# A fused Fourier-filter and ELU-MLP kernel: order of the k2 = 0 products and place of one unit's sums, against buffers, engines and places of the opening's last pieces

## The chip, the cores and the metric

One NeuronCore of a Trainium2 chip runs the whole kernel in one launch. The metric is the device time of one execution in microseconds (us); lower is better. The engines are PE (TensorE; PEld is its weight loads), DVE (VectorE), ACT (ScalarE), POOL (GpSimd) and SP (SyncE, which here only issues DMAs). ACT and POOL issue DMAs as well.

## The reference, cut to what matters

```python
# x: (8, 3008, 256) float32; filt_r, filt_i: (1505, 256) float32
X = np.fft.rfft(x, axis=1)
y = np.fft.irfft(X * (filt_r + 1j * filt_i)[None], n=3008, axis=1).astype(np.float32)
t = y.reshape(8 * 3008, 256)
h = t @ w_in                                  # w_in: (256, 2048) float64
g = np.where(h > 0.0, h, np.exp(np.minimum(h, 0.0)) - 1.0)
out = (g @ w_out).astype(np.float32)          # w_out: (2048, 256) float64
```

A real Fourier transform over 3008 positions, a product with a filter for each frequency and channel, the transform back, and then a two-layer network with ELU between the layers.

## The kernel before, in words

**Transform.** 3008 = 47 x 64, so each transform is done in two steps, with tables of sines and cosines as matmul weights: forward `a_unit` (64) and `b_unit` (47, then the products with the filter on DVE), back `bi_unit` (47) and `n_unit` (64). Between them the intermediate results go through DRAM: `z_write` and `z_read` before `b_unit`, `y_write` and `y_read` (tensor `yd`) before `n_unit`. A batch b has 8 groups g of 4 frequencies k2, and 6 units m of output positions. From the second batch on, `bi_unit` takes two groups at once: 16 products of 32x32 tiles of PE, with row strip 32a and column strip 32p for a, p = 0 to 3, whose inputs (`zs`, z) GpSimd has added up in lines 385 to 395. For g = 0 the frequency k2 = 0 needs weights of its own, so each of the four tiles with a = 0 does two products of half the width (lines 405 to 411). Before, these come as: the four special halves, the twelve other tiles, the four ordinary halves. ACT copies the four results out (line 412).

**The first batch** has forms of its own, `a_first`, `t_first`, `b_first`, `bi_first`, `y_write_first`, which keep the data on the core as far as they can. `bi_first` (line 347) puts the result of group g into one half, g % 2, of one tile `t3f`; ACT fills it (lines 356, 357) and `y_write_first` writes it to `yd` by two DMAs (line 364), for the last group one of them from ACT's queue. Then `y_read(0, 0)` (line 430), two DMAs from SP and two from ACT, reads what `n_unit(0, 0)` needs (line 443 on PE, line 445 the copies by ACT).

**Network.** Both layers multiply in seven products in place of eight, on blocks of two by two. `combine` (lines 469 to 472) forms the sums of the input blocks of one unit on DVE. An item is (b, m, q), q a quarter of the hidden width. `up_steps` does seven products of two matmuls each (line 494), with copies by ACT (line 505) and adds by DVE (line 502), ELU by two ACT operations (lines 511, 512) and one of DVE (line 516), and at the end four sums on DVE (lines 552 to 556). `down_steps` does the seven products of the second layer one item later (line 576). `c_unit` (line 592) combines those of four quarters on DVE, `o_unit` turns them and writes them out.

**Weights.** They arrive as 64-bit numbers in 16 pieces k = 0 to 15 and are turned into 32-bit ones on the core: `w_fetch` (DMA, line 650), `w_split` (DVE, lines 662, 663), `w_float` (ACT: lines 670, 671 and, in `w_power`, 678, 679), `w_join` (DVE, lines 685 to 698). After each second piece `w_sums` (lines 706 to 709) forms the block sums of four operations on DVE. The 15th piece is k = 14; pieces 14 and 15 use the same working tiles.

**Order.** Everything is issued in an order written out by hand; each engine does its own instructions in the order in which the program names them, and waits where data or a buffer is not yet free. After the opening a loop runs over quads i: quad i holds the up steps of item i and the down steps of item i - 1, mixed by a string of U and D. A table `plan` holds what else is issued: at place 0, after the first four up steps, or at place 1, after the tails of the quad. Batch b begins at quad (b - 1) * 24, and unit m = 5 has its first up step at 44 behind that. In that loop before, `n_unit` of m = 5 comes at quad 40, place 0, and its sums, split off as `n_sums`, at quad 41, place 1; the other units have both at one place. PSUM has four banks that all these units share in turn and four for the second layer.

Of the kernel before, what the change touches and what calls it, by code (L numbers as in the profile page):

```python
# [11 lines left out]
FP32 = mybir.dt.float32  # L12
U32 = mybir.dt.uint32
AXT = mybir.ActivationFunctionType
ALU = mybir.AluOpType
# [11 lines left out]
P = 128  # L27
D = 256
# [6 lines left out]
NG = K2 // 4  # L35
# [93 lines left out]
def kernel(  # L129
# [9 lines left out]
    nc = tc.nc  # L139
# [6 lines left out]
    def pool(name, bufs, **kw):  # L146
        return ctx.enter_context(tc.tile_pool(name=name, bufs=bufs, **kw))
# [7 lines left out]
    t2p = pool("t2p", 2)  # L155
# [13 lines left out]
    bb = pairs[:, P:3 * P].rearrange("p (v a i) -> p v a i", v=2, a=4)  # L169
# [8 lines left out]
    xs, tas, tns, t1s, t2s, ss, t3s, t4s, zs, yds, ys, g_of, po_of, cs_, sds = ({} for _ in range(15))  # L178
# [8 lines left out]
    def bank(name, shape=(P, 2, D)):  # L187
        i = banks.pop(0)
        return i, psM.tile(list(shape), FP32, tag="m%d" % i, name=name)
# [156 lines left out]

    def bi_first(g):
        s = ss.pop((0, g))
        t = t3s[0, g] = t3f[:, g % 2]

        pa, pb = (psO.tile([P, 2, 256], FP32, tag="po%d" % i, name="po%d" % i)
                  for i in ((0, 1) if g > 2 and g % 2 else (2, 3)))
        for o, table, sv in ((0, gr, s[0]), (64, gi, s[1])):
            for ps, k in ((pa, LO), (pb, HI)):
                tile_mm(ps[o:o + 64], table, k, sv, g == 0 and k == LO)
        nc.scalar.activation(out=t[:, 0:2, :], in_=pa, func=AXT.Copy)
        nc.scalar.activation(out=t[:, 2:4, :], in_=pb, func=AXT.Copy)
# [41 lines left out]
    def bi_unit(b, g):  # L399
        z = ss.pop((b, g))  # L400
        t = t3s[b, g] = t3p.tile([P, 2, 4, D], FP32, tag="t3", name="t3")
        pv = [bank("pv") for _ in range(4)]

        both = [(p, a, slice(1 if g == a == 0 else 0, 2), 0) for p in range(4) for a in range(4)]
        if g == 0:
            both = [(p, 0, slice(0, 1), 1) for p in range(4)] + [w for w in both if w[1]] + [w for w in both if not w[1]]
        for p, a, js, v in both:
            r = slice(32 * a, 32 * a + 24)
            nc.tensor.matmul(pv[a][1][32 * p:32 * p + 32, js, :], bb[r, v, p, :], z[r, p, js, :],  # L409
                             start=True, stop=True, tile_position=(32 * a, 32 * p))  # L410
        for a, (i, ps) in enumerate(pv):
            nc.scalar.activation(out=t[:, :, a, :], in_=ps, func=AXT.Copy)
            banks.append(i)
# [22 lines left out]
    def n_unit(b, m):  # L436
        t, w, h = t4s.pop((b, m)), tns.pop((b, m)), half(m)
        rows = []
        for dh in range(2):
            y = yp.tile([P, 512], FP32, tag="y%d" % dh, name="y%d" % dh)  # L440
            k, ps = bank("psn", (P, 512))
            for q, i in enumerate(order(m)):
                nc.tensor.matmul(ps[:, ts(q, P)], t[:, i - 4 * m, ds(dh * P, P)], w[:, i - 4 * m, :],  # L443
                                 start=True, stop=True)
            nc.scalar.activation(out=y[:, 0:2 * h], in_=ps[:, 0:2 * h], func=AXT.Copy)
            banks.append(k)
            rows += [y[:, 0:h], y[:, h:2 * h]]
        s = yp.tile([P, 3, 256], FP32, tag="ys", name="ys")
        ys[b, m] = rows + [s[:, i, 0:h] for i in range(3)]

    def n_sums(b, m):
        ys[b, m] = combine(*ys[b, m])

# [11 lines left out]
    def combine(b11, b12, b21, b22, t1, t2, t4):  # L467

        nc.vector.tensor_tensor(out=t1, in0=b12, in1=b11, op=ALU.subtract)
        nc.vector.tensor_tensor(out=b12, in0=b22, in1=b12, op=ALU.subtract)  # L470
        nc.vector.tensor_tensor(out=t2, in0=b22, in1=t1, op=ALU.subtract)
        nc.vector.tensor_tensor(out=t4, in0=b21, in1=t2, op=ALU.subtract)
        return {1: b11, 2: b21, 3: b22, 4: t4, 5: t1, 6: t2, 7: b12}
# [191 lines left out]
    def w_float(k, part=None):  # L665
        m, e, f, l = wts[k]
        if part == 1:
            return w_power(e)

        nc.scalar.activation(out=l, in_=wds[k][:, :, 0], func=AXT.Identity, scale=2.0 ** -52)  # L670
        nc.scalar.activation(out=f, in_=m, func=AXT.Identity, scale=2.0 ** -20, bias=1.0)
        if part is None:
            w_power(e)
# [7 lines left out]
    def w_join(k):  # L681
        q, j = divmod(k, 4)
        m, e, f, l = wts.pop(k)
        hi = wds.pop(k)[:, :, 1]
        nc.vector.scalar_tensor_tensor(out=e, in0=hi, scalar=0x80000000, in1=e,
                                       op0=ALU.bitwise_and, op1=ALU.bitwise_or)
        nc.vector.tensor_tensor(out=f, in0=f, in1=l, op=ALU.add)
        e = e.bitcast(FP32)
        if j < 2:
            f, e = (t.rearrange("p (a j c) -> p a j c", a=2, j=2) for t in (f, e))  # L690
            dst = w_in[q][:, 2 * j:2 * j + 2, :, :].rearrange("p j a c -> p a j c")
            nc.vector.tensor_tensor(out=dst, in0=f, in1=e, op=ALU.mult)
        else:

            f, e = (t.rearrange("p (i a e s) -> p i e a s", i=2, a=4, e=2) for t in (f, e))
            dst = w_out[q][:, 0:4, j - 2, :].rearrange("p (i e) (a s) -> p i e a s", i=2, a=4)
            for i in range(2):
                nc.vector.tensor_tensor(out=dst[:, i], in0=f[:, i], in1=e[:, i], op=ALU.mult)
        if j % 2 == 1 and k < 15:
            w_sums(k)  # L700

    def w_sums(k):
        q, j = divmod(k, 4)
        w = (w_in if j < 2 else w_out)[q]
        a11, a21, a12, a22, s1, s2, s4 = (w[:, i] for i in range(7))
        nc.vector.tensor_tensor(out=s1, in0=a21, in1=a22, op=ALU.add)
        nc.vector.tensor_tensor(out=s2, in0=s1, in1=a11, op=ALU.subtract)
        nc.vector.tensor_tensor(out=s4, in0=a12, in1=s2, op=ALU.subtract)
        nc.vector.tensor_tensor(out=a21, in0=a11, in1=a21, op=ALU.subtract)

    def f_arrange():

# [27 lines left out]
    with tc.manual_schedule():  # L740


        with tc.tile_pool(name="boot", bufs=1) as bp:
# [9 lines left out]
            t3f = t3p.tile([P, 2, 4, D], FP32, tag="t3", name="t3")  # L753
# [86 lines left out]
            w_join(12)  # L840
            w_fetch(15)
            w_split(14)
            w_float(14)
            w_join(13)
        for c in range(2):
            x_load(1, c)
# [2 lines left out]
        ep = pool("ep", 2)  # L849
        op = pool("op", 1)  # L850
        n_unit(0, 0)
        n_sums(0, 0)
        w_join(14)

# [3 lines left out]
        def at(quad, place, fn, *a):  # L860
            plan.setdefault((quad, place), []).append((fn, a))


        for quad, place, fn, *a in ((0, 0, w_split, 15), (1, 1, w_float, 15, 0), (2, 0, w_float, 15, 1), (2, 1, w_join, 15),
                                    (3, 0, w_sums, 15)):
            at(quad, place, fn, *a)
        for c in range(2, XBUFS):
# [7 lines left out]
        for b in range(B):  # L875
            t = (b - 1) * PER
            if b > 0:
                for c, s in enumerate((2, 2, 4, 4, 7, 7)):
                    at(t + s, 0, x_unit, b, c)
                    if c % 2 == 0:  # L880
                        opens.add(t + s + 1)
                        at(t + s, 1, a_unit, b, c)
                    nb, nxt = (b, c + XBUFS) if c + XBUFS < NXC else (b + 1, c + XBUFS - NXC)
                    if nb < B:
                        at(t + s, 1, x_load, nb, nxt)
                    at(t + s, 1, z_write, b, c)
                for g in range(NG):
                    s = t + 9 + g + g // 2
                    at(s, 1, b_unit, b, g)
                    at(s - 2, 1, f_read, b, g)  # L890
                    at(s - 2, 1, z_read, b, g)
                    if g % 2:

                        opens.add(s + 2)
                        at(s + 1, 1, bi_unit, b, g - 1)
                        at(s + 1, 1, y_write, b, g - 1)
            for m, (s, place) in enumerate(((23, 0), (25, 1), (29, 1), (32, 0), (36, 0), (40, 0))):
                if b > 0 or m > 0:
                    at(t + s - 2, 0, tn_read, b, m)
                    at(t + s - 2, 0, y_read, b, m)  # L900
                    at(t + s, place, n_unit, b, m)

                    at(*((t + s + 1, 1) if m == 5 else (t + s, place)), n_sums, b, m)
                at(t + PER + 4 * m + 5, 0, c_unit, b, m)
                at(t + PER + 4 * m + 6, 0, o_unit, b, m)

        items = [(b, m, q) for b in range(B) for m in range(6) for q in range(4)]
        for i in range(-PER, len(items) + 3):
# [3 lines left out]
            for k in "DUUDUDDU" if i in opens else "UUDUDDU":  # L912
                s = ups if k == "U" else downs
# [4 lines left out]
            for k in "DUUDUD" if i in opens else "DUUDUDD":  # L918
                s = ups if k == "U" else downs
# [40 lines left out]
```

## Time and profile before

| | us |
|---|---|
| three runs | 2618.73, 2620.72, 2621.56 |
| median | 2620.72 |
| the profiled execution | 2620.72 |
| its span, first to last instruction | 2618.7 |
| busy: PE / DVE / ACT / POOL | 2569.9 / 1852.8 / 1504.0 / 486.9 |
| 20 us stretches of the opening, PE busy: 60 to 80, 80 to 100 | 16.55, 9.95 |
| granted PE clock in those | 0.83, 0.76 |

The profile is of one execution. Times in it count from the span's start. Matmuls are pipelined and their ends are modelled, so a busy PE is not PE at its peak; a line of the timeline gives the start, the duration, the engine, the source line and what is written and read, xN merges N records, and square brackets give the engine's idle time before and what ended it. A float32 matmul is two passes, so two records, each with a weight load of its own. Lines of the list of waits read: who waited for whom, us in total, times, longest. In the chain of waits each piece is what the next one had to wait for.

### The profile page before, as it was taken

The numbers are of one execution on the slowest core, as the hardware profiler recorded it, in microseconds if no ns is written. First come the engines' busy times: TensorE is split into PE (matmuls) and PEld (weight loads), VectorE is DVE, ScalarE is ACT, GpSimd is POOL, SyncE is SP. The second block draws the span as 40 slices with busy tenths as digits, with TensorE's granted clock in tenths as the row PEclk, the third lists the DMA queues.
The fourth block names the chain that finished last, engine by engine and source line by source line (L and its number), as shares of the span: only waits on it lengthen the run. The fifth ranks groups of instructions, "written<-read, shape, count | busy, mean of one in ns | idle before, by whom it ended". The sixth has DMA issues, their size and how long they took to land.

```text
span 2618.7 us, 41226 instructions
## 1 busy us (share of the span) xinstructions
PE 2569.9 (98%) x15300; PEld 2220.2 (85%) x15300; DVE 1852.8 (71%) x3203; ACT 1504.0 (57%) x2622; POOL 486.9 (19%) x669
## 2 busy tenths in 40 slices
PE   6799999999999999999999999999999999999998
PEld 4688889888898888988889888998889888898887
DVE  6876776677666776777667767677677667766666
ACT  7665555655555555555555555555555555555554
POOL 5102330024100331004300134002330023300000
PEclk9899999999999999999999999999999999999999
DMA  9544222432224232333314331143321332210010
GB/s 296 169 115 105 63 63 55 117 83 70 66 62 115 63 92 48 82 90 80 79 45 104 83 98 45 45 111 96 86 61 40 87 85 63 63 41 20 22 28 17
DMA packets 228840, 206.51 MB, mean 79 GB/s; under 512 B 130962, under 2 KB 194674, under 8 KB 228640
## 3 DMA queue, kind: packets, MB, share of 16 engines
q1 hardware_dynamic: 211328, 166.90, 25.4%
q0 software_dynamic: 15856, 36.25, 4.9%
q8 instruction: 121, 1.98, 0.3%
q10 hardware_dynamic: 1456, 0.72, 0.1%
q14 instruction: 79, 0.65, 0.1%
HBM read 131.91 MB, written 78.17 MB: 80 GB/s over the span
## 4 chain that ended last, share of the span: by engine, by line
PE 96%; DMA 0%; DVE 0%; ACT 0%; issue 0%; DVEq 0%; SPq 0%; ACTq 0%
PE po L576 44%; PE phs L494 25%; PE phd L494 12%; PE pha L494 6%; PE psn L443 3%; PE psr L376 2%; PE psa L228 2%; PE pv L409 1%; PE po L324 0%; DMA yd<-t 0%; PE psi L376 0%; DMA t<-yd 0%; PE psr L324 0%; DVE c L592 0%; PE psi L324 0%
## 5 line engine op out<-in xcount | busy, mean ns | idle before, releaser
L576 PE MATMUL po<-g,wo 128*128 128x256 f32 (+1 forms) x5376 | 1306.1, 376 | 0.0
L576 PEld LDWEIGHTS po<-g,wo 128*128 128x128 f32 x5376 | 1016.2, 190 | 139.1 <-issue 20.0
L505 ACT ACTIVATE g<-phs 128x512 f32<-128x512 f32 (+1 forms) x576 | 339.3, 589 | 819.2 <-PE phs L494 819.1
L502 DVE TENSOR_TENSOR g<-phd,g 128x512 f32<-128x512 f32 (+1 forms) x384 | 259.4, 675 | 413.3 <-ACT e L512 322.2
L512 ACT ACTIVATE e<-e 128x512 f32<-128x512 f32 (+1 forms) x768 | 477.2, 621 | 24.3
L516 DVE SCALAR_TENSOR_TENSOR g<-e,g 128x512 f32<-128x512 f32 (+1 forms) x576 | 400.5, 695 | 1.3 <-ACT e L512 1.3
L494 PE MATMUL phs<-y,wi 128*128 128x256 f32 (+1 forms) x1536 | 394.5, 380 | 0.0
L494 PE MATMUL phs<-ys,wi 128*128 128x256 f32 (+1 forms) x1536 | 387.9, 375 | 1.5 <-ACT g L505 1.5
L511 ACT ACTIVATE e<-g 128x512 f32<-128x512 f32 (+1 forms) x576 | 353.2, 613 | 35.7 <-DVE g L502 26.6
L494 PEld LDWEIGHTS phs<-y,wi 128*128 128x128 f32 x1536 | 284.9, 191 | 55.1 <-issue 11.5
L494 PEld LDWEIGHTS phs<-ys,wi 128*128 128x128 f32 x1536 | 291.9, 190 | 34.9 <-ACT g L505 2.5
L385 POOL TENSOR_TENSOR sr<-sr,zs 128x512 f32<-128x512 f32 x56 | 71.3, 1273 | 1131.7 <-DVE zs L330 1131.7
L516 DVE SCALAR_TENSOR_TENSOR g<-e,phs 128x512 f32<-128x512 f32 (+1 forms) x192 | 129.9, 677 | 128.5 <-ACT e L512 128.5
L511 ACT ACTIVATE e<-phs 128x512 f32<-128x512 f32 (+1 forms) x192 | 112.9, 588 | 147.7 <-PE phs L494 147.7
L494 PE MATMUL phd<-ys,wi 128*128 128x256 f32 (+1 forms) x768 | 194.6, 376 | 0.0
L494 PE MATMUL phd<-y,wi 128*128 128x256 f32 (+1 forms) x768 | 193.8, 375 | 0.0
L494 PE MATMUL pha<-y,wi 128*128 128x256 f32 (+1 forms) x768 | 193.8, 375 | 0.0
L494 PEld LDWEIGHTS phd<-ys,wi 128*128 128x128 f32 x768 | 145.4, 190 | 19.0 <-DVE g L502 3.0
L494 PEld LDWEIGHTS pha<-y,wi 128*128 128x128 f32 x768 | 146.1, 190 | 16.3
L494 PEld LDWEIGHTS phd<-y,wi 128*128 128x128 f32 x768 | 146.1, 190 | 16.2
L502 DVE TENSOR_TENSOR g<-pha,g 128x512 f32<-128x512 f32 (+1 forms) x192 | 129.2, 673 | 40.5 <-PE pha L494 40.2
L553 DVE TENSOR_TENSOR g<-g,g 128x512 f32<-128x512 f32 (+1 forms) x192 | 130.7, 681 | 6.7
(129 smaller groups left out, 2356.5 us busy)
## 6 DMA issues: line engine op xcount, KB each, us to landing
yd<-t SPq DMA_DIRECT2D x127, 192.0 KB
t<-yd SPq DMA_DIRECT2D x190, 128.0 KB
z<-t SPq DMA_DIRECT2D x84, 256.0 KB
f<-fp POOLq DMA_DIRECT2D x224, 96.0 KB, 3.1
t<-z SPq DMA_DIRECT2D x224, 96.0 KB
out_dram<-o SPq DMA_DIRECT2D x632, 32.0 KB
tn<-tn_t SPq DMA_DIRECT2D x48, 256.0 KB
xc<-in_x_dram SPq DMA_DIRECT2D x84, 128.0 KB
```

The source lines that it names most:

```text
L228: nc.tensor.matmul(p[o:o + 64, u, :], w[r, u, o:o + 64], src[r, u, :], start=True, stop=True)
L376: nc.tensor.matmul(ps[32 * a:32 * a + 32, c, :], fb[k, 1 if g == a == 0 else 0, c, :], t[k, a, :], start=True, stop=True)
L385: nc.gpsimd.tensor_tensor(out=sr, in0=sr, in1=p, op=ALU.add)
L443: nc.tensor.matmul(ps[:, ts(q, P)], t[:, i - 4 * m, ds(dh * P, P)], w[:, i - 4 * m, :], start=True, stop=True)
L494: nc.tensor.matmul(ps[:, a, 0:h], w_in[q][:, COMBO[n], a, :], y[n], start=start and a == 0, stop=True, skip_group_check=True)
L502: nc.vector.tensor_tensor(out=g[o], in0=i0, in1=i1, op=ALU.add)
L505: nc.scalar.activation(out=g[o], in_=i0, func=AXT.Copy)
L511: nc.scalar.activation(out=e, in_=src, func=AXT.Relu, scale=-1.0)
L512: nc.scalar.activation(out=e, in_=e, func=AXT.Exp, scale=-1.0)
L516: nc.vector.scalar_tensor_tensor(out=g[n], in0=es[n], scalar=1.0, in1=src, op0=ALU.subtract, op1=ALU.max)
L553: nc.vector.tensor_tensor(out=b12, in0=b22, in1=b12, op=ALU.subtract)
L576: nc.tensor.matmul(po[i][:, u, 0:h], w_out[q][:, COMBO[n], a, :], g[n][:, a, :], start=q == 0 and a == 0 and n in (1, 3, 6, 4), stop=True, ...
```

## The change

It does two things at once. It puts in new places for the end of the opening, and it takes back an order of the k2 = 0 products and a split of the sums of the unit m = 5.

- `bi_first`: for g = 6 and 7 the result goes into a tile of its own from the pool `t2p`, not into a half of `t3f`.
- `w_sums`: pieces 11, 13 and 15 on GpSimd, the earlier ones on DVE as before.
- Piece 14: the last two ACT operations of `w_float` move from ahead of `n_unit(0, 0)` to quad 0, place 0; `w_join(14)` from behind the first unit's sums to quad 0, place 1; `w_split(15)` from quad 0, place 0, to quad 1, place 0.
- `bi_unit`: the products in order of p and then a, the two halves of a tile with a = 0 next to each other.
- `n_unit`: the sums are part of it again; for m = 5 all of it comes at quad 41, place 0, and its reads (`tn_read`, `y_read`) at quad 39 in place of 38.

```diff
     def bi_first(g):
         s = ss.pop((0, g))
-        t = t3s[0, g] = t3f[:, g % 2]
+        t = t3s[0, g] = t3f[:, g % 2] if g < NG - 2 else t2p.tile([P, 4, D], FP32, tag="t2", name="t3")
...
-        both = [(p, a, slice(1 if g == a == 0 else 0, 2), 0) for p in range(4) for a in range(4)]
-        if g == 0:
-            both = [(p, 0, slice(0, 1), 1) for p in range(4)] + [w for w in both if w[1]] + [w for w in both if not w[1]]
-        for p, a, js, v in both:
-            r = slice(32 * a, 32 * a + 24)
-            nc.tensor.matmul(pv[a][1][32 * p:32 * p + 32, js, :], bb[r, v, p, :], z[r, p, js, :],
-                             start=True, stop=True, tile_position=(32 * a, 32 * p))
+        for p in range(4):
+            for a, (_, ps) in enumerate(pv):
+                for js, v in ((slice(0, 1), 1), (slice(1, 2), 0)) if g == a == 0 else ((slice(0, 2), 0),):
+                    r = slice(32 * a, 32 * a + 24)
+                    nc.tensor.matmul(ps[32 * p:32 * p + 32, js, :], bb[r, v, p, :], z[r, p, js, :],
+                                     start=True, stop=True, tile_position=(32 * a, 32 * p))
...
-        ys[b, m] = rows + [s[:, i, 0:h] for i in range(3)]
-
-    def n_sums(b, m):
-        ys[b, m] = combine(*ys[b, m])
+        ys[b, m] = combine(*rows, *(s[:, i, 0:h] for i in range(3)))
...
-        nc.vector.tensor_tensor(out=s1, in0=a21, in1=a22, op=ALU.add)
+        queue = nc.vector if k < 11 else nc.gpsimd
+        queue.tensor_tensor(out=s1, in0=a21, in1=a22, op=ALU.add)
...
-            w_float(14)
+            w_float(14, 0)
             w_join(13)
...
         n_unit(0, 0)
-        n_sums(0, 0)
-        w_join(14)
...
-        for quad, place, fn, *a in ((0, 0, w_split, 15), (1, 1, w_float, 15, 0), (2, 0, w_float, 15, 1), (2, 1, w_join, 15),
+        for quad, place, fn, *a in ((0, 0, w_float, 14, 1), (0, 1, w_join, 14), (1, 0, w_split, 15), (1, 1, w_float, 15, 0), (2, 0, w_float, 15, 1), (2, 1, w_join, 15),
                                     (3, 0, w_sums, 15)):
...
-            for m, (s, place) in enumerate(((23, 0), (25, 1), (29, 1), (32, 0), (36, 0), (40, 0))):
+            for m, (s, place) in enumerate(((23, 0), (25, 1), (29, 1), (32, 0), (36, 0), (41, 0))):
...
-                    at(*((t + s + 1, 1) if m == 5 else (t + s, place)), n_sums, b, m)
```

More of the change, by code (lines that the diff above doesn't have):

```diff
@@ L705, in w_sums @@
         a11, a21, a12, a22, s1, s2, s4 = (w[:, i] for i in range(7))
-        nc.vector.tensor_tensor(out=s1, in0=a21, in1=a22, op=ALU.add)
-        nc.vector.tensor_tensor(out=s2, in0=s1, in1=a11, op=ALU.subtract)
-        nc.vector.tensor_tensor(out=s4, in0=a12, in1=s2, op=ALU.subtract)
-        nc.vector.tensor_tensor(out=a21, in0=a11, in1=a21, op=ALU.subtract)
+        queue = nc.vector if k < 11 else nc.gpsimd
+        queue.tensor_tensor(out=s1, in0=a21, in1=a22, op=ALU.add)
+        queue.tensor_tensor(out=s2, in0=s1, in1=a11, op=ALU.subtract)
+        queue.tensor_tensor(out=s4, in0=a12, in1=s2, op=ALU.subtract)
+        queue.tensor_tensor(out=a21, in0=a11, in1=a21, op=ALU.subtract)
     def f_arrange():
```

## The prediction

> **What bounds the kernel now.** I read the page first: its busy list, and the chain of work that ended last. PE (TensorE) is busy 98% of the span, and the chain lies on PE for 96%. Then the table by stage, for the long stretch behind the opening, and the list of waits for the opening.
>
> ```profile
> PE 2569.9 (98%) x15300; PEld 2220.2 (85%) x15300; DVE 1852.8 (71%) x3203; ACT 1504.0 (57%) x2622; POOL 486.9 (19%) x669
> ...
> PE 96%; DMA 0%; DVE 0%; ACT 0%; issue 0%; DVEq 0%; SPq 0%; ACTq 0%
> ```
>
> ```profile
> 120.00:2600.00 2480.00, 2480.00 (x14776) 2151.34 (x14776) 1754.52 (x3013) 1418.90 (x2471) 443.58 (x587) 1.00 0.28 71
> ```
>
> The first pair of numbers behind the stretch is its length and PE's busy time: equal. From 120 us on PE has no gap at all, and its list of waits there is empty. So two questions decide: how much earlier or later does PE become continuously busy (the opening), and how much PE time is added behind it. Whatever another engine saves after 120 us is worth nothing.
>
> In the opening the longest wait is PE's 10.1 us for the first unit of the step back (line 443). The chain leads to it:
>
> ```profile
> 82.50 0.60 ACT t L357
> ...
> 83.47 3.63 DMA yd<-t
> ...
> 87.21 0.04 ACT t L356
> ...
> 87.70 0.60 ACT t L357
> ...
> 88.32 3.07 DMA yd<-t
> ...
> 91.97 3.72 DMA t<-yd
> ...
> 95.93 3.75 PE psn L443 x16
> ```
>
> Read downwards: the last eviction (g = 7) starts at 87.21 because its half of the shared tile is still being written out by the transfer of g = 5, which lands at 87.10. Its own result is then written (landed 91.39) and read back (95.69).
>
> **1. Results of g = 6 and 7 in other places.** Removed: that wait, which ended ACT's 2.39 us without work. What is late next: PE's products for g = 7. Evictions of g = 5 and 6, both released by PE, start 1.72 us apart (82.01, 83.73), so g = 7 can start at 85.45, when ACT is free (84.81): 1.76 us earlier. The write-out then overlaps the two of g = 6, still under way until about 88 by the DMA shares; both ends are no delay and 0.8 us (half a write's 3.07 us shared for half of it); I take 0.35. ACT's half of the read back stands behind the four ACT operations of piece 12, whose second (line 671) waits for `w_split(12)` on DVE. That now comes first on DVE, at 87.9 and not 89.52, because the sums of piece 11 are gone from DVE, so the read back's issue keeps up. If GpSimd's sums slow it (line 663 took 0.83 us and not 0.42 beside a GpSimd memset at 94.3), 0.4 to 0.9 us of the gain go. **Sum: -1.4 us, between -1.8 and -0.3.**
>
> The granted clock takes part of it back. It is 0.50 from 90.2 to 100.4 and 1.00 from 100.6 in the table by stage, 4.6 us after PE's restart at 95.93; after the earlier idle time PE restarted at 70.15 and the clock rose at 76.6, 6.5 us later. If the point of change does not move along with the restart, 1.4 us of PE work run at half rate, part of them behind ACT anyway. **+0.3, between 0 and 0.8.** The Trainium skill (TensorE: Matmul & The Clock Gate, "What's actually happening") says that the window which decides is free-running, 3.4 us long, and does not start with the kernel; the two delays do not contradict it, and by it this term would differ from run to run.
>
> **2. Sums of pieces 11, 13 and 15 on GpSimd.** Twelve operations of 128x256: 0.42 us each on DVE (line 706), 0.73 to 1.25 us on GpSimd (lines 386, 390), 3 to 5 us for four. Those of 11 and 13 are first used in quad 3, some 40 us later. Those of 15 can start when `w_join(15)` ends, 136.3, and PE's first use is at 146.78: at most 5 of 10 us. On GpSimd's queue they push what stands behind them: the memset of `x_load`, then the filter's rearranging DMAs. The first six of these go from 94.8 to about 99, the second six from 106.8 to about 140 and land by about 158; the filter is first read at 174.61. Cover of 16 us: **0**. Without it, the first filter step at 223 would be late by the excess.
>
> **3. The 15th piece spread.** `w_float(14)` loses its last two ACT operations ahead of the first unit. Nothing is won there: ACT was done at 97.23 and the first results of line 443 came at 98.0. They go into quad 0, between the two halves of its steps. There ACT is the path:
>
> ```profile
> 105.29 0.58 ACT L512 ACTIVATE e<-e 128x448 f32<-128x448 f32 x1
> 105.90 0.54 ACT L511 ACTIVATE e<-phs 128x448 f32<-128x448 f32 x1
> ...
> 109.37 0.53 ACT L505 ACTIVATE g<-phs 128x448 f32<-128x448 f32 x1
> ```
>
> ```profile
> 109.94 1.02 PE L494 MATMUL phs<-ys,wi 128*128 128x224 f32 x4 [0.90 <-ACT g L505]
> ```
>
> From 104.25 to 109.9 ACT has no gap beyond 0.15 us, and PE waits for its last one. The same two operations of piece 15 take 1.37 us from the first to what follows (127.18 to 128.55). So PE's wait grows from 0.90 to about 2.3: **+1.4 us, between 1.0 and 1.4.** `w_join(14)`, 2.1 us on DVE, moves from before the first add (there DVE waited for PE at 105.07 anyway) to the end of quad 0, where 2.61 us of DVE's idle time before line 502 at 114.86 take it; `w_split(15)` follows it into what is left: 0.
>
> **4. The unit m = 5 and its sums, a quad later.** Its PE and ACT work only moves; it is used three quads on. Its five DMA issues on SP move behind the four writes and four reads of a step back and come 13 us later, two quads before use: 0. Its sums now follow `c_unit` on DVE in quad 17 (about 327 to 332 us for the first batch), where line 502 already starts at 329.48 without idle time. I work out a DVE delay there of 1 us against 0.9 us of slack at PE's fourth product: **+0.5 us over eight batches, between 0 and 3.**
>
> **5. The k2 = 0 products in the other order.** This is the term that decides. Seven times (b = 1 to 7), 20 matmuls run on 16 tiles of 32x32. The four tiles with a = 0 have two matmuls each. Before, these pairs are pulled apart: four, then the twelve others, then four. After, both halves stand next to each other. The row before, with what follows it, and an ordinary one of 16:
>
> ```profile
> 249.66 1.29 PE L409 MATMUL pv<-zs,pairs 24*32 24x256 f32 x40
> 250.88 1.13 PE L576 MATMUL po<-g,wo 128*128 128x256 f32 x4
> ```
>
> ```profile
> 291.83 1.14 PE L409 MATMUL pv<-zs,pairs 24*32 24x512 f32 x32
> 292.90 1.13 PE L576 MATMUL po<-g,wo 128*128 128x256 f32 x4
> ```
>
> From the first start to the next line: 1.22 and 1.07 us. Each matmul is two passes. Starts on one tile are 0.22 us apart for 256 columns (line 376: 236.36, 236.59, 236.81, 237.02) and 0.45 for 512; different tiles start 7 ns apart, so a waiting second pass does not hold up other tiles. But there is a limit. In the row of 40, the passes of all 16 first matmuls are issued freely, 32 in number; of the last four matmuls, the first starts its passes at 0.46 and 0.67 us on a tile just free, while the other three, whose tiles have long been free, start only at 0.65 to 0.68, just after the record of the first matmul's second pass ends at 0.61. I read that as 32 passes outstanding, given free in order when they end.
>
> After, the head of the line is one tile's four passes in a row: starts 0, 0.24, 0.46, 0.67. The first 32 passes reach to the first half of a = 0, p = 3. The six passes of its last three tiles get their places only as the head ends (0.61, 0.83, 1.05, then freely): the last first pass starts at about 1.13, its second at 1.58, and as in the ordinary row 0.5 us later the next line begins: 2.07 us. Worked on the two rows above this rule gives 1.18 and 1.06. **+0.85 us each, +5.9 us in seven.** Bounds: if nothing limits what is outstanding, 16 pairs end like the ordinary row, -0.15 each, **-1.1**; if each second half holds back all behind it, four times 0.46 us go by before the last tiles start, 2.9 in all, +1.65 each, **+11.6**. I take the middle because it alone gives the delay of the three late starts.
>
> The Trainium skill (TensorE: Matmul & The Clock Gate, "Architectural detail") gives PE a queue of 64 entries, and in "Step-by-step: what each phase is for" says that only weight loads are pulled ahead and "the MATMULs themselves stay in program order". The depth agrees with 32 passes of a weight load and a matmul each. Strict order differs from the rows: 16 first passes start within 0.1 us while their second passes wait 0.45. By strict order the term would be its upper end, +11.6; by the rows it is 5.9, and the rows decide.
>
> **Sum:** -1.4 + 0.3 + 1.4 + 0.5 + 5.9 = +6.7. The profiled execution took 2620.72 us (span 2618.7 and 2.0 around it), the same as the median of the three runs, so **2627.4**. About 0.2%, 5.2 us, is what a measurement of this kernel can tell from no change.
>
> **Rivals.**
> - *The order costs nothing* (22%): PE takes the pairs as it takes sixteen. For it: all tiles start 7 ns apart. Against it: the three late starts. Then -1.4 + 0.3 + 1.4 + 0.5 - 1.1 = -0.3, **2620.4, not slower**. It decides as soon as a product row of k2 = 0 stays under 1.2 us.
> - *Strict order* (9%): +11.6 in place of 5.9, **2633.1**. For it, the 0.46 us that a pair needs; against it, the 7 ns.
> - *The opening gives nothing* (8%): the read back stays bound to piece 12 behind a slowed `w_split(12)`, or the overlapped writes land no earlier. Then **2628.8**. This is also the way in which the change does not do what it says.
> - *The opening gives all and ACT's two operations are hidden* (3%) with the order for free: about 2618; faster by 0.2% is hardly in reach, since the waits of PE ahead of 120 us that the change touches are 10.1 us, mostly one transfer chain.
>
> The forecast has 58%, with an own range of 2625 to 2630. **Range 2620 to 2631**: it takes in most of the first rival, leaves out strict order and the lowest. Chances: slower by over 0.2%: 0.45 of the forecast's 0.58, strict order 0.09, the opening for nothing 0.08, together 0.62; within 0.2%: the forecast's other 0.13 and 0.21 of the first rival, 0.34; faster: 0.04.
>
> **What will show it.** Right: the k2 = 0 product rows about 2.07 us to the next line, seven times; PE without other gaps from 122 us on; the eviction of g = 7 at about 85.5 and without a DMA wait; line 443 first at 94 to 95; in quad 0 lines 678/679 between two of 512 and 511, and PE's wait of about 2.3 us for line 505. Wrong: product rows at 1.2 or 2.9; PE waiting in quad 17 by over 0.3 us; PE waiting for GpSimd at line 576 in quad 4.

## The result, and the profile after

Four runs of the changed kernel took 2634.14, 2634.59, 2635.87 and 2638.45 us, median **2635.23**; four of the kernel before beside them 2619.72 in the median (2618.72 to 2621.56). The ratio is 1.006, interval 1.0043 to 1.0078: slower by some 15.5 us. The forecast was 2627.4, its range ended at 2631. The direction was right, the size was not: over half of the loss was missing.

The profiled execution is the one of 2638.45 (span 2636.6), the slowest of the four and 17.7 us over the profiled one of before. Lines from 409 to 445 carry numbers one lower than before, those from 469 to 698 four lower: 498 is the add of before's 502, 572 the second layer of 576, 465 to 468 the `combine` of 469 to 472.

First the two views that bounded the kernel before: busy time and chain from the page, then the long stretch in the table by stage.

```profile
PE 2581.3 (98%) x15300; PEld 2219.9 (84%) x15300; DVE 1858.8 (70%) x3191; ACT 1505.8 (57%) x2622; POOL 497.8 (19%) x681
...
PE 95%; DVE 2%; DMA 2%; ACT 1%; issue 0%; SPq 0%; DVEq 0%; ACTq 0%
```

```profile
120.00:2600.00 2480.00, 2473.02 (x14715) 2137.33 (x14715) 1755.20 (x2999) 1414.53 (x2461) 452.16 (x598) 1.00 0.29 71
```

PE is no longer busy without a gap behind the opening: 2473.02 of 2480.00, so 7.0 us of gaps, and DVE has come into the chain with 2%. PE's list of waits from 66 us to the end names them (in all, times, longest):

```profile
PE psn L442 <- DMA t<-yd: 9.3, 1, 9.3
PE phd L490 <- DVE g L498: 7.0, 7, 1.0
PE phs L490 <- ACT g L501: 2.7, 2, 2.1
PE psr L324 <- DVE si L329: 0.2, 1, 0.2
```

The first was 10.1 before and the third 1.5 (longest 0.9). The fourth was 3.3 before, but executions with the opening of before show 0.2, 1.3 and 3.3, so nothing is read from it. The second is new: once in each of seven batches PE waits 1.0 us for an add of DVE. The first of the seven in the timeline, and the first k2 = 0 row:

```profile
334.06 1.03 PE L572 MATMUL po<-g,wo 128*128 128x256 f32 x4
336.09 1.13 PE L490 MATMUL phd<-ys,wi 128*128 128x256 f32 x4 [1.00 <-DVE g L498]
```

```profile
252.82 2.13 PE L408 MATMUL pv<-zs,pairs 24*32 24x256 f32 x40
254.88 1.13 PE L572 MATMUL po<-g,wo 128*128 128x256 f32 x4
```

Three places hold the loss. The k2 = 0 row takes 2.06 us to the next line in place of 1.22, in all seven batches: +5.9. From one such row to a product of its batch behind quad 17 it is 86.06 us in place of 83.95; 0.84 of the 2.11 is the row itself, so the wait and PE's new start behind it cost 1.27: times seven, +8.9. And the first k2 = 0 row starts at 252.82 in place of 249.66: the opening lost 3.2 in this execution. Together 18.0 of 17.7 us.

### The profile page after: what moved, and what is told of

Read it like the earlier page. It is cut to its first block, busy times and chain, and to the rows that moved or that the text cites. A ratio compares the mean times of both kernels' runs of the same rounds, so it can differ in the third digit from the quotient of the medians.

```text
span 2636.6 us, 41237 instructions
## 1 busy us (share of the span) xinstructions
PE 2581.3 (98%) x15300; PEld 2219.9 (84%) x15300; DVE 1858.8 (70%) x3191; ACT 1505.8 (57%) x2622; POOL 497.8 (19%) x681
## 4 chain that ended last, share of the span: by engine, by line
PE 95%; DVE 2%; DMA 2%; ACT 1%; issue 0%; SPq 0%; DVEq 0%; ACTq 0%
PE po L572 43%; PE phs L490 25%; PE phd L490 12%; PE pha L490 6%; PE psn L442 3%; PE psr L377 2%; PE psa L228 2%; PE pv L408 1%; DMA wd<-in_moe_w_in_dram 1%; DMA wd<-in_moe_w_out_dram 1%; DMA xc<-in_x_dram 0%; PE po L324 0%; DVE ys L465 0%; DVE ys L467 0%; PE psi L377 0%
```

## The experiments

All but two start from the kernel before. Each is compared with runs of the kernel before on the same chip; the differences of medians are given beside the ratio with its interval.

### The order alone

```diff
-        both = [(p, a, slice(1 if g == a == 0 else 0, 2), 0) for p in range(4) for a in range(4)]
...
+        for p in range(4):
+            for a, (_, ps) in enumerate(pv):
+                for js, v in ((slice(0, 1), 1), (slice(1, 2), 0)) if g == a == 0 else ((slice(0, 2), 0),):
```

> The kernel before with the changed order of the k2 = 0 products alone. My theory (places for 32 passes, given free in order): seven product rows of 2.07 us to the next line in place of 1.23, +0.84 each, so +5.9 us in all (+0.22%), no other wait of PE changed. Rival (the rows cost time on paper only, PE makes it up behind them): rows of 2.07 but a time within 1.5 us of the kernel before. Rival (strict order of matmuls): rows of 2.9, +11.6 us.

2627.72 (11 runs) against 2621.42: +6.3, ratio 1.0023 (1.0015 to 1.0032). All seven rows take 2.07 us, the distance from one to the next grew from 316.40 to 317.24, and PE has no wait behind the opening. That is the forecast's term, in size and place. The single records of the changed kernel's first row show the working too: its last six passes start 0.86, 1.08, 1.10, 1.28, 1.53 and 1.55 us after its first one, the same here within 0.01. The prediction had worked out 1.13 for the last first pass and 1.58 for its second.

### The second halves in the middle

The order of before, but the four ordinary halves come after the first four of the twelve other tiles: a case that neither kernel has.

```diff
-... + [w for w in both if w[1]] + [w for w in both if not w[1]]
+... + [w for w in both if w[1] == 1] + [w for w in both if not w[1]] + [w for w in both if w[1] > 1]
```

> The kernel before with the second halves of the four tiles a = 0 placed after the first four of the twelve others and not at the end. Nothing is left out. My theory (32 passes outstanding, places given free in order as passes end): the last eight tiles get their places only as the head's passes end; worked out with the rates of the rows before, 1.63 us in the rule, so 1.65 to 1.7 us from the first start to the next line, and +3 us in all. Rival (tiles take what is theirs whatever the order, only adjacent halves hurt): 1.07 to 1.23. Rival (strict order, a half on a busy tile holds up all behind it): the first of the second halves can start at 0.46, the eight others after about 0.7, so 1.2 to 1.7 depending on what counts as held; above 1.9 would refute both rules.

A single execution took 2624.0, which by itself tells nothing; the row can be read. The timeline has it and the next line:

```profile
249.83 1.72 PE L409 MATMUL pv<-zs,pairs 24*32 24x256 f32 x40
251.48 1.13 PE L576 MATMUL po<-g,wo 128*128 128x256 f32 x4
```

1.65 us from start to start, as worked out beforehand from 32 passes outstanding whose places come free in order when they end; 316.8 us from batch to batch. The rule was read from the row of before (1.22) and has then given 2.07 and 1.65 us for two other orders of the same twenty matmuls. That does not prove the mechanism, but both rivals of the prediction are out by the 2.07: an order for free (1.07) and strict order (2.9). The 1.65 alone would not tell the rule from strict order, for which 1.2 to 1.7 was expected here.

### The unit m = 5 alone

```diff
-            for m, (s, place) in enumerate(((23, 0), (25, 1), (29, 1), (32, 0), (36, 0), (40, 0))):
+            for m, (s, place) in enumerate(((23, 0), (25, 1), (29, 1), (32, 0), (36, 0), (41, 0))):
...
-                    at(*((t + s + 1, 1) if m == 5 else (t + s, place)), n_sums, b, m)
+                    at(t + s, place, n_sums, b, m)
```

> The kernel before with the unit m = 5 and its sums at quad 41, place 0, alone. My theory now, from the changed kernel's list of waits (PE waited seven times 1.0 us for DVE line 498): the sums run beside GpSimd's adds, take 3.2 us and not 1.7, hold up DVE's next add from PSUM and so PE's fourth product; seven waits of about 1.0, with refilling 1.27 us each, +8.9 us. Rival (the waits need the late opening or the long product rows of the changed kernel): no waits here, within 1.5 us.

2629.95 (5 runs): +8.5, ratio 1.0036 (1.0022 to 1.0049). PE's list of waits has the new line with nothing else of the change there:

```profile
PE phd L494 <- DVE g L502: 6.9, 7, 1.0
```

So the wait belongs to this step, and it is the larger half of the loss.

### The unit there, its sums one place later

The unit's products, copies and reads move as in the change; only the sums stay where they were, at quad 41, place 1.

```diff
-... (36, 0), (40, 0))):
+... (36, 0), (41, 0))):
...
-                    at(*((t + s + 1, 1) if m == 5 else (t + s, place)), n_sums, b, m)
+                    at(t + s, 1 if m == 5 else place, n_sums, b, m)
```

> The kernel before with the unit m = 5 at quad 41, place 0, as in the change, but with its sums still apart, at quad 41, place 1, where they were before. Theory (DVE's adds beside GpSimd's, ahead of the add that PE waits for, make the seven waits of 1.0 us): DVE's order is that of before, the seven waits for line 502 are gone, and the distance from one k2 = 0 row to the next is that of before, 316.40 us within 0.3; the time is that of before, +0 to +2 us, where the upper end is ACT's four copies in quad 17 making PE wait for ACT by up to 0.3 us a batch. Rival (the unit's own products, copies and reads in quad 17 make part of the wait): distance 317 or more, +4 to +8.9 us.

2621.48 (11 runs) against 2621.22: ratio 1.0002 (0.9993 to 1.0011). The waits for line 502 are gone; the rows are 316.4 us apart. Moving the unit costs nothing that can be measured. What costs is DVE's four sums standing ahead of the add that PE needs next.

### GpSimd's adds left out beside them

Why do four sums of 0.42 us delay DVE so much? DVE's timeline of the changed kernel in quad 17, and GpSimd's of the same time:

```profile
329.56 0.52 DVE L588 TENSOR_TENSOR k<-k,c 128x256 f32<-128x256 f32 x1
330.12 0.84 DVE L588 TENSOR_TENSOR c<-c,k 128x256 f32<-128x256 f32 x1
330.88 0.41 DVE L588 TENSOR_TENSOR c<-po,k 128x256 f32<-128x256 f32 x1
...
332.18 1.06 DVE L465 TENSOR_TENSOR ys<-y 128x256 f32<-128x256 f32 x1 [0.35 <-ACT y L444]
333.34 0.76 DVE L466 TENSOR_TENSOR y<-y,y 128x256 f32<-128x256 f32 x1
334.03 0.94 DVE L467 TENSOR_TENSOR ys<-y,ys 128x256 f32<-128x256 f32 x1
335.01 0.42 DVE L468 TENSOR_TENSOR ys<-y,ys 128x256 f32<-128x256 f32 x1
335.35 0.68 DVE L498 TENSOR_TENSOR g<-phd,g 128x512 f32<-128x512 f32 x1
```

```profile
331.51 1.44 POOL L389 TENSOR_TENSOR si<-si,zs 128x512 f32<-128x512 f32 x1
333.03 0.79 POOL L390 TENSOR_TENSOR zs<-si 128x256 f32<-128x256 f32 x1
333.78 0.90 POOL L391 TENSOR_TENSOR zs<-si 128x256 f32<-128x256 f32 x1
```

While GpSimd adds up the inputs of a later double step, three of the four sums take 0.76 to 1.06 us; the fourth, behind GpSimd's last add (ended 334.68), takes 0.42. From the start of line 465 to that of the add it is 3.17 us. The next experiment takes the changed kernel and leaves out GpSimd's six adds for g = 5 (batches 1 to 7), so that part of the step back for those frequencies is not computed:

```diff
+        if g != 5:
-        nc.gpsimd.tensor_tensor(out=sr, in0=sr, in1=p, op=ALU.add)
+            nc.gpsimd.tensor_tensor(out=sr, in0=sr, in1=p, op=ALU.add)
...
```

> The changed kernel without GpSimd's six adds for g = 5 (lines 386 to 391), batches 1 to 7: this part of the computation is left out, all else stays. My theory: it is these adds, running beside the sums of the unit m = 5, that stretch the sums (0.76 to 1.06 us each in place of 0.42). Without them the four take about 1.7 us, DVE's add from PSUM starts about 333.7 in place of 335.35, and PE's seven waits of 1.0 us at line 490 are gone: 8 to 9 us less than the changed kernel (2635.2), so about 2626.5. Rival (the sums are late because c_unit stands ahead of them, or because ACT's copies come late): the waits stay at 0.8 to 1.0 each.

2629.67 (6 runs) against 2621.59: +8.1, ratio 1.0032 (1.002 to 1.0044). PE's waits for line 499 (the same add) are gone. The same stretch of DVE:

```profile
331.65 0.43 DVE L466 TENSOR_TENSOR ys<-y 128x256 f32<-128x256 f32 x1 [1.07 <-ACT y L445]
332.18 0.42 DVE L467 TENSOR_TENSOR y<-y,y 128x256 f32<-128x256 f32 x1
332.52 0.42 DVE L468 TENSOR_TENSOR ys<-y,ys 128x256 f32<-128x256 f32 x1
332.97 0.42 DVE L469 TENSOR_TENSOR ys<-y,ys 128x256 f32<-128x256 f32 x1
333.31 0.68 DVE L499 TENSOR_TENSOR g<-phd,g 128x512 f32<-128x512 f32 x1
```

1.66 us in place of 3.17. PE takes the product that needs this add at 334.39, and the add ends at 333.99: not even the delay of DVE that the undisturbed sums make reaches PE, with 0.4 us to spare. When the sums start is not behind the difference: in both kernels the first one starts 2.50 us after the unit's products (329.68 to 332.18, and 329.15 to 331.65), held by ACT's copy. The extra 1.51 us less these 0.4 give 1.1, against the wait of 1.0 that was seen. So GpSimd's adds beside the sums are the cause of the wait. The trace is shorter by 1.26 us in each of seven batches (317.24 from row to row, as with the order alone), 8.8 in all; against the runs of before beside each, the loss fell from 15.5 to 8.1 us, 7.4, which four and six runs do not tell from 8.8. The 8.1 that are left answer to the order alone (+6.3) and the opening alone (+1.1, below).

### The sums at the unit's old place

```diff
-                    at(*((t + s + 1, 1) if m == 5 else (t + s, place)), n_sums, b, m)
+                    at(t + s, place, n_sums, b, m)
```

> The kernel before, unit m = 5 left at quad 40, place 0, but its sums there as well and not split off. My theory: in that quad DVE has 4.0 us without work ahead of its add from PSUM (311.5 to 316.2 for the first batch) and GpSimd's adds run at other times, so the sums fit: no waits of PE, time within 1.5 us of the kernel before. Rival (any place 0 in this stretch is too full): waits of about 1 us, +7 to 9 us.

A miss: 2626.23 (10 runs), +4.6, ratio 1.0016 (1.0006 to 1.0025). PE waits seven times here too:

```profile
PE phd L494 <- DVE g L502: 2.7, 7, 0.4
```

I had expected GpSimd's adds at other times. But those of the group g = 4 run beside quad 16's place 0 (310.05 to 315.79), as those of g = 5 do in quad 17, and the sums take 0.44, 0.76, 0.94 and 0.42 us there. The wait is 0.4 us and not 1.0; the next experiment shows by what.

### c_unit behind the sums

The changed kernel, with `c_unit` of m = 3 one place later.

```diff
-                at(t + PER + 4 * m + 5, 0, c_unit, b, m)
+                at(t + PER + 4 * m + 5, 1 if m == 3 else 0, c_unit, b, m)
```

> The changed kernel with c_unit of m = 3 moved from place 0 to place 1 of the same quad, so that the sums of m = 5 are the first thing on DVE there. My theory: DVE sat idle 0.35 us before the first sum, waiting for ACT's copy, so c_unit is not what holds the sums up; waits stay, 0.8 to 1.0 us each, time within 2 us of the changed kernel. Rival (c_unit's 1.9 us ahead of the sums is the cause): waits gone or below 0.3, 6 to 9 us less.

A miss by far: 2703.25 (4 runs), ratio 1.0312 (1.0295 to 1.033) against the kernel before, and 68 us over the changed kernel's median. The list of waits shows the reason:

```profile
PE po L572 <- DVE c L588: 40.4, 8, 5.1
...
PE phd L490 <- DVE g L498: 4.0, 7, 0.6
```

`c_unit` empties the banks of the second layer, and PE's next down steps wait for them 5.1 us, eight times. Each such gap also brings the granted clock down to 0.50. In the first batch the table by stage, in slices of 1 us, has 0.50 from 341 to 350 us and 1.00 from 351; PE is busy again from 342.51, so some 8 us of its work run at half speed and cost 4 more. From the first k2 = 0 row to the second it is 327.15 us in place of 318.50: 8.65 more (5.04 of wait and 4 of half speed, less 0.43 by which the other wait is shorter), and eight gaps of about that make up the 68.

What I wanted to know is in the second line: without `c_unit` ahead of them the sums still make PE wait 0.6 us, less than the 0.8 to 1.0 expected. The four kernels together show by what. From the first sum to DVE's next add it is 3.17 us in the changed kernel, 2.74 here, 2.55 with the sums at the old place and 1.66 without GpSimd's adds; PE waits 1.00, 0.57, 0.38 and 0 us. Each of the three waits is 2.17 less than its stretch, and the three stretches differ in the first sum alone (1.06, 0.63 and 0.44 us). So the wait follows the length of the sums, and `c_unit` matters at most by when the first of them meets GpSimd's adds.

### The opening, whole and in parts

Whole (all edits of the opening):

> The kernel before with all edits of the opening (tiles of their own for g = 6 and 7, sums of pieces 11, 13, 15 on GpSimd, piece 14 spread) and nothing else. My theory: the rest of the sum, that is -0.4 to -1.4 us ahead of the first unit and +1.2 to 1.5 in quad 0, with up to 1.4 more if the granted clock falls again after PE's longer wait there: between 0 and +3 us. Rival (what the record forecast for the opening without a second fall of the clock): +0.3. If the three parts do not add up to the +15.5 measured, something between them was missed.

Without the spread of piece 14 (own tiles and sums on GpSimd):

> The kernel before with the two tiles of their own and the three GpSimd sums, but piece 14 left where it was. My theory: the spreading is what costs in the opening, so without it PE's wait in quad 0 is 0.9 us as before, and the time is 0.4 to 1.4 us below the kernel before. Rival (GpSimd's sums slow DVE and take the gain): equal to the kernel before or up to 1 us above.

The own tiles for g = 6 and 7 alone:

> The kernel before with own tiles for the results of g = 6 and 7 and nothing else. Theory (the two transfers after one another set the start of PE's stage, the sums of piece 11 on DVE don't): PE's wait for the first unit falls from 10.1 to about 8.8 us as in the two runs that had the sums on GpSimd too, and the time is 1 to 1.6 us under before. Rival (the read back is issued by ACT behind the operations of piece 12, which wait for DVE's sums of piece 11): the wait stays at 9.6 us or more, and the time is within 0.6 us of before. The start of that stage differs by 2 us between executions, so the wait is read, not the start.

The spread alone:

> The kernel before with piece 14 spread into quad 0 and nothing else of the change. Theory: PE's wait for ACT in quad 0 is 2.1 us in place of 0.9, and the granted clock falls to 0.50 once more for about 3 us behind it, together +2.6 us: 2.2 to 3 us over before. Rival (the fall of the clock belongs to the earlier start of PE's stage and not to the longer wait): the wait of 2.1 us is there without the fall, +1.2 us.

The edits are those of the diff at the top, hunk by hunk.

| kernel, 11 runs each | median | before | ratio, interval | PE's wait for the first unit | longest wait for ACT |
|---|---|---|---|---|---|
| whole | 2622.53 | 2621.42 | 1.0005 (0.9996 to 1.0014) | 8.9 | 2.1 |
| without the spread | 2619.82 | 2621.42 | 0.9994 (0.9985 to 1.0002) | 8.7 | 0.9 |
| own tiles alone | 2620.33 | 2621.22 | 1.0 (0.9991 to 1.0009) | 9.8 | 0.9 |
| spread alone | 2622.66 | 2621.22 | 1.0007 (0.9998 to 1.0016) | 9.9 | 2.1 |

No ratio can be told from 1 by itself; the waits can be read, since each is one line of one list.

*Own tiles alone: the rival is right by the wait.* It falls only from 10.1 to 9.8, and executions with the opening of before show 9.9 to 10.2; the time, 0.9 us less, cannot be told from none. The chain of that run:

```profile
86.16 0.34 DVE wo L709
86.50 0.35 DVE wm L662
...
86.87 0.63 ACT wfl L671
87.50 0.62 ACT we L678
...
88.14 0.04 ACT we L679
...
88.74 3.70 DMA t<-yd
```

The read back is issued by ACT behind piece 12, which waits for `w_split(12)`, which waits for the sums of piece 11 on DVE. Only when these go to GpSimd too does the wait fall, to 8.7 to 9.5 in the five kernels with both edits: the two belong together.

*Spread alone: the rival's sign came here too.* PE waits 2.1 us for ACT, but in this execution the clock stays up. Both kernels in the table by stage, from the restart behind that wait; the third number from the right is the granted clock. First the changed kernel (PE starts again at 111.43):

```profile
112.00:115.20 3.20, 3.20 (x10) 2.86 (x9) 3.06 (x7) 0.55 (x1) 0.00 (x0) 0.50 1.04 321
```

and the spread alone (restart at 109.91):

```profile
110.40:113.60 3.20, 3.20 (x18) 3.20 (x17) 3.06 (x7) 0.91 (x2) 0.00 (x0) 1.00 1.06 314
```

In slices of 0.8 us the clock of the changed kernel rises at 101.70, falls at 111.94 and rises at 115.36: distances of 3 times 3.41 and of 3.42. Laid on such a grid, its whole gap (109.31 to 111.43) lies in one step (108.53 to 111.94), and so does that of the whole opening. In the run with the spread alone the grid from its rise at 99.10 puts an edge at 109.34 into the gap (107.79 to 109.91): 1.55 and 0.57 us idle in two steps, and no fall. This fits what the Trainium skill says (TensorE: Matmul & The Clock Gate, "What's actually happening"): a free-running window of 3.4 us decides. Its table lets the clock fall after an idle window; here 2.12 us idle of 3.41 were enough, in two executions. How much idle time it takes is open. The two other kernels with this gap kept their clock: with `c_unit` behind the sums the gap (110.80 to 112.92) splits into 0.74 and 1.38 us (rise at 101.30, edge at 111.54), and without GpSimd's adds (110.45 to 112.57) into 1.97 and 0.15 (rise at 102.18, edge at 112.42), so if idle time within a step decides, the limit lies between 1.97 and 2.12, which no run was made to test. The fall costs 1.35 us in the next line (line 572 in 112.61 to 115.64: 3.03 us for 8 records, 1.68 before) and 0.4 in the one ahead of it, in those executions that it hits.

## Why the prediction was wrong in size

**Step 4 failed**: "I work out a DVE delay there of 1 us against 0.9 us of slack", and so 0.5 us over eight batches, with 3 as the upper end. It measured 8.9 (trace) and 8.5 (by itself); PE waiting in quad 17 by over 0.3 us was named there as a sign of being wrong. By the rows the slack was 0.76 us: in the kernel before the add of line 502 ended at 330.16, and PE took its product at 330.92. The delay was 1.87: in the changed kernel the add ended at 336.03, 1.11 after the 334.92 at which PE would have come to it (0.86 behind the line before). The list of what stands ahead of line 502 on DVE was right; the durations were not. I took each sum at 0.42 us, its mean at its old place, and did not ask what GpSimd does in quad 17. The trace of before already had the sign, in four adds of line 592 that ran there beside GpSimd's:

```profile
327.29 0.52 DVE L592 TENSOR_TENSOR k<-k,c 128x256 f32<-128x256 f32 x1
327.85 0.84 DVE L592 TENSOR_TENSOR c<-c,k 128x256 f32<-128x256 f32 x1
328.61 0.41 DVE L592 TENSOR_TENSOR c<-po,k 128x256 f32<-128x256 f32 x1
328.95 0.61 DVE L592 TENSOR_TENSOR c<-k,k 128x256 f32<-128x256 f32 x1
329.48 0.68 DVE L502 TENSOR_TENSOR g<-phd,g 128x512 f32<-128x512 f32 x1
```

```profile
327.61 0.80 POOL L386 TENSOR_TENSOR zs<-sr 128x256 f32<-128x256 f32 x1
328.36 0.92 POOL L387 TENSOR_TENSOR zs<-sr 128x256 f32<-128x256 f32 x1
329.24 1.44 POOL L388 TENSOR_TENSOR si<-si,zs 128x512 f32<-128x512 f32 x1
```

```profile
330.92 1.03 PE L494 MATMUL phd<-ys,wi 128*128 128x256 f32 x4
```

The Trainium skill (SBUF — State Buffer, "Who interferes with whom") has the rule that I did not weigh: a DVE instruction with two inputs in SBUF contends with a GpSimd instruction that reads SBUF; by the same page's "Summary: rules for kernel authors" the second to issue waits until the first finishes. The rows agree: in the changed kernel the two engines' instructions end in turn (GpSimd 332.95, DVE 333.24, GpSimd 333.82, DVE 334.10, GpSimd 334.68, DVE 334.97), and line 588's add that reads PSUM (`c<-po,k`) keeps its 0.41 us amid GpSimd's adds.

**Step 5 was right**: 2.07 us a row, +5.9 in all; alone +6.3 (interval 3.9 to 8.4).

**Step 1 was right in the mechanism and too high in the gain.** The chain now runs from PE's products into the eviction of g = 7 at 85.80, without a DMA ahead of it (357 and 358 are 356 and 357 of before):

```profile
85.80 0.60 ACT t L357
86.40 0.53 ACT t L358
...
86.94 4.07 DMA yd<-t
...
91.69 3.60 DMA t<-yd
...
95.54 3.75 PE psn L442 x16
```

The eviction follows that of g = 6 by 1.72 us in place of 3.48: the 1.76 forecast. The write took 4.07 us in place of 3.07, beside the two of g = 6: 1.0 more, where I had allowed 0.35. PE's restart came 0.4 us earlier in this execution, and the wait was 0.8 shorter (0.6, 1.2, 1.3 and 1.4 in the four other kernels with these edits), against 1.4 forecast. The clock rose at 101.7 in place of 100.5 though PE started earlier: 0.8 us lost, the upper end of that term.

**Step 2** was nothing for PE behind the opening, as forecast. But GpSimd's sums of piece 11 stretched the four operations of `w_split(12)` and `w_split(13)` from 0.42 us each to 0.42, 0.95, 0.95 and 0.95: the loss within step 1 that was named there. In the kernel without the spread the chain of waits runs through it: over line 663 of piece 12 (0.88 us in the chain) and ACT's lines 678 and 679 to the read back.

**Step 3** was right in the wait: 2.12 us for a forecast of about 2.3, +1.2. The second fall of the clock, up to 1.7 us behind it, was not thought of. With it the opening's loss in the profiled execution adds up: -0.4, +0.8, +1.2 and +1.7 are 3.3, of 3.2.

The parts by themselves, +6.3, +8.5 and +1.1, sum to 15.9; the whole change measured 15.5. They do not act on one another to any amount that shows, within intervals of some us.

Open is whether the opening without the spread is a gain: 1.6 us in the median, interval from 0.15% faster to 0.02% slower. No kernel here beats the one before beyond doubt.

## What to carry to other kernels

Before putting small DVE work ahead of an instruction that the bound engine waits for, look at GpSimd's timeline for the same microseconds: four adds of 0.42 us took 3.2 us there and made PE wait 1.0, and one place later they cost nothing. Where several matmuls of one tile follow each other while other tiles run beside it, pull them apart in the program; counting 32 passes outstanding, and not tiles, told the length of the row in the two orders tried here. And read a gap of PE together with the clock behind it: 2 us of waiting cost up to 1.7 more, depending on where they fall.

## What the runs showed that was not expected

- The same gap of 2.1 us brought the granted clock to 0.50 for 3.4 us in two of five executions, the two in which it lay whole in one step of a grid of 3.41 us.
- The start of PE's long stretch differs between executions of the same opening: the first unit's products came at 95.93 in the kernel before, at 94.15 and 92.22 in the order alone and in the unit alone, which share its opening. One execution does not resolve an edit of 1 us there; the wait in front does.
- GpSimd is slowed in turn: its add of 128x512 (line 389) took 1.44 us where it began during the last add of line 588, and the one of line 386 took 1.27.
